# Stores of the w2 and w1 sums moved to ScalarE's queue, w2 loaded in one transfer, and the sums spread anew over the token tiles

## The chip, the cores and the metric

The kernel runs on one core of one Trainium2 chip. That core has five engines, each with an instruction stream of its own that it works through in order: TensorE (PE, with its weight loads shown as PEld), VectorE (DVE), ScalarE (ACT), GpSimd (POOL) and SyncE (SP, which here only issues transfers). Sixteen DMA engines move data between the chip's HBM and the core's SBUF. The metric is the device time of one execution in microseconds.

## The reference, cut to what matters

```python
x = A_x                                   # (1, 2048, 576)
xn = _layernorm(x)
q, k, v = split(xn @ wqkv)                # 32 heads of 18
phi = lambda t: where(t > 0, t + 1, exp(t)) + 1e-6
kv = einsum("bhsd,bhse->bhde", phi(k), v)
z  = einsum("bhsd->bhd", phi(k))
s  = (phi(q) @ kv / (phi(q) . z + 1e-6)) @ wo
g  = silu(gelu(xn @ w1 + b1) @ w2 + b2)   # w1 (576, 4608), w2 (4608, 576)
return x + s * g
```

Everything is float32. The kernel keeps that accuracy by writing each operand as a high part and a low part of a faster 32-bit format and multiplying high by high, high by low and low by high.

## The kernel before: how it is tiled and staged

The work runs in three stages.

**Projection stage** (L547 to L663). A loop over 16 token tiles of 128 tokens. Tile t computes the key columns `pk` (28 products, L315), then adds the outer product of the tile before to the running state (`state`, L381: 10 products into `ps_kva`, `ps_kvb`), then computes the rest of the value columns `pv` (14 products). Tiles 0 to 5 are normalized and transposed on the core. From tile 6 on, transposed x is loaded (`xt`, L260), the tile's mean and scale are stored to HBM by `store_stats` (L264) and read back to all partitions by `load_stats` (`bc`, L269), then POOL subtracts the mean (`center`, L278), DVE multiplies by the scale (`scale`, L281), ACT writes the high part (`set_x_hi`, L289) and DVE the low part (`set_x_lo`, L293, L294). `set_x_hi` of tile t+1 stands in iteration t, and the key products of tile t+1 wait for it. After tile 15 the query weights follow (`split_w` of `wq`, L357, L358, then `query(0)`).

**Attention stage** (L1076 to L1111) and **feed-forward stage** (L1512 to L1609). The feed-forward multiplies with two-level block sums (a Strassen-like scheme), which need sums of blocks of w1 and w2.

Some of those sums are made beside the projection stage, and the change is about these:

- w2 has nine *places* c = 0 to 8, each with four blocks of 128 x 2 x 288 numbers. `w2_load` (L393) brings a place in as two transfers: three blocks in a tile `w2r` (864 KB), the fourth in a tile `w2u` (288 KB), two buffers each.
- Each place has three sums, numbered 5, 6 and 4 and made in that order: `w2_sum` on POOL (L410), the high part by `w2_hi` on ACT (L419), the low part by `w2_lo` on DVE (L423), then `w2_store` (L427) writes both parts, 576 KB, to HBM. The parts stand in a tile `w2o`, of which there are four in turn (`w2slot`), so the high part of a sum waits for the store of the fourth sum before it.
- The last 64 rows of w1 come in five groups q: `we_load` (L439), `we_sums` on POOL (L444), `we_hi` on ACT (L450), `we_lo` on DVE (L454), `we_store` (L458, 896 KB). They use the buffers `w1u` and `w1h`, which later become the x tiles of block 3: `set_x_hi(12)` waits for the last `we_store`.
- Three tables say when. `W2_SUMS[t]` lists the sums that POOL makes at the end of iteration t. Their high and low parts and their stores follow in iteration t+1, the stores at its end. `W2_LOADS[t]` is the place loaded at the end of iteration t. `WE_SUMS` does the same for w1's rows, in iterations 1, 3, 5, 7 and 9.

**What sets the order.** `ordered` (L526) keeps each engine's instructions as written. All transfers are issued from SP, in program order. A transfer of the kernel signals on one of eight completion counters, handed out in turn, and waits before it is issued until the one eight transfers earlier on the same counter has landed. In the built program this is a wait on each transfer's own counter.

## Time and profile before

| | us |
|---|---|
| median of 3 runs | 1112.03 (1110.18 to 1114.05) |
| the profiled execution | 1111.23 |
| its span, from first to last instruction | 1109.4 |
| PE busy | 1092.8 |
| DVE busy | 811.6 |
| ACT busy | 489.1 |
| POOL busy | 453.0 |

The granted TensorE clock was full all through (1.0). The profile's numbers are microseconds from the start of the span. A group row gives engine, line, operation and tiles, then count and durations; "SPq" is SP's queue of issued transfers, whose duration is that of issuing. A waits row reads: engine and line, what it waited for, then total, number of times and the longest. A stretches row gives for each engine the busy time and the number of instructions in it, then the granted clock, the mean busy share of the 16 DMA engines (small overlaps take it over 1) and the rate in GB/s.

### The profile page before, as it was taken

What the parts mean: (1) busy time and instruction counts of PE and PEld (TensorE: products, weight loads), DVE (VectorE), ACT (ScalarE), POOL (GpSimd) and SP (SyncE); (2) the same over time, 40 slices, a digit from 0 to 9 for tenths busy, and PEclk for the clock granted to TensorE, in tenths of its full rate; (3) what the DMA queues carried; (4) which work ended last, traced back from release to release, by engine and by line L of the source; (5) the groups of instructions that cost most, each with busy time, mean ns of one, the idle gap of its engine ahead of it and who ended that gap; (6) DMA issues with size and microseconds to landing.
All of it is one profiled execution on the core that took longest, in us unless ns stands there. A gap on an engine that the chain in (4) does not pass through costs nothing.

```text
span 1109.4 us, 18111 instructions
## 1 busy us (share of the span) xinstructions
PE 1092.8 (98%) x6712; PEld 1008.9 (91%) x6712; DVE 811.6 (73%) x1132; ACT 489.1 (44%) x848; POOL 453.0 (41%) x392
## 2 busy tenths in 40 slices
PE   8998989999999999999999999999999999999998
PEld 8998888999998989989989899898898998989988
DVE  7586667888687888877879788676485674765866
ACT  6654466464554454443544544524233242242342
POOL 3566564232352453534624534325234242341340
PEclk9999999999999999999999999999999999999999
DMA  8799883475879577585585769987766676766452
GB/s 257 254 285 298 279 342 133 142 244 182 293 267 336 195 262 261 188 326 204 210 319 189 284 241 378 403 296 255 232 221 229 207 237 208 248 219 206 140 186 86
DMA packets 90272, 270.17 MB, mean 244 GB/s; under 512 B 11846, under 2 KB 23878, under 8 KB 87496
## 3 DMA queue, kind: packets, MB, share of 16 engines
q1 hardware_dynamic: 90184, 269.02, 70.4%
q8 instruction: 53, 0.87, 0.3%
q14 instruction: 35, 0.29, 0.1%
HBM read 171.28 MB, written 95.76 MB: 241 GB/s over the span
## 4 chain that ended last, share of the span: by engine, by line
PE 87%; DMA 6%; DVE 3%; ACT 1%; issue 1%; POOL 1%; SPq 0%; DVEq 0%; POOLq 0%
PE pm L1287 34%; PE a L1153 10%; PE e L1153 10%; PE zy L1153 10%; PE ps_s L795 5%; PE pq L315 5%; PE b L1153 5%; DMA op<-w2o 2%; PE pd L1403 2%; PE pk L315 1%; DMA bc<-st_dram 1%; DVE w2o L423 1%; PE pv L315 1%; PE ptp L777 1%; DMA w2r<-w 1%
## 5 line engine op out<-in xcount | busy, mean ns | idle before, releaser
L1293 DVE TENSOR_TENSOR macc<-pm,macc 128x576 f32<-128x576 f32 x218 | 163.9, 752 | 54.5 <-PE pm L1287 53.7
L819 ACT CAST h_h<-g 128x512 fp32r<-128x512 f32 x204 | 120.8, 621 | 132.4 <-PE pm L1287 131.3
L822 DVE TENSOR_TENSOR h_l<-g,h_h 128x512 fp32r<-128x512 f32 x204 | 165.0, 816 | 0.0
L1253 POOL TENSOR_TENSOR mid<-g 128x512 f32<-128x512 f32 x34 | 43.9, 1290 | 127.7 <-ACT g L1161 127.7
L1247 POOL TENSOR_TENSOR g<-g 128x512 f32<-128x512 f32 x34 | 55.1, 1622 | 56.6 <-DVE h_l L822 55.3
L1161 ACT ACTIVATE g<-b,b1c 128x512 f32<-128x512 f32 x36 | 24.7, 687 | 116.0 <-DVE b L1179 116.0
L1170 ACT COPY mid<-a 128x512 f32<-128x512 f32 x36 | 21.1, 587 | 117.2 <-PE a L1153 117.2
L865 POOL TENSOR_TENSOR w1raw<-w1raw 128x256 f32<-128x256 f32 x18 | 16.9, 938 | 121.6 <-DVE wa L881 121.6
L1173 DVE TENSOR_TENSOR mid<-b,mid 128x512 f32<-128x512 f32 x36 | 24.7, 687 | 44.6 <-PE b L1153 43.1
L1250 POOL TENSOR_TENSOR g<-g 128x512 f32<-128x512 f32 x34 | 55.2, 1623 | 2.7
L1375 POOL TENSOR_TENSOR fin1l<-fin1h,fin1l 128x288 f32<-128x288 f32 x8 | 6.5, 810 | 118.9 <-DMA fin1l<-s_dram 104.5
L1153 PE MATMUL a<-h0r,wa 128*128 128x512 f32 x144 | 50.4, 390 | 0.0
L1153 PE MATMUL a<-xh,wa 128*128 128x512 f32 x144 | 50.4, 390 | 0.0
L822 DVE TENSOR_TENSOR h_l<-mid,h_h 128x512 fp32r<-128x512 f32 x34 | 48.8, 1437 | 1.2
L1244 POOL TENSOR_TENSOR g<-g 128x512 f32<-128x512 f32 x34 | 46.7, 1372 | 2.7
L1179 DVE TENSOR_TENSOR b<-e,mid 128x512 f32<-128x512 f32 x36 | 25.2, 699 | 30.4 <-PE e L1153 30.4
L760 POOL TENSOR_TENSOR pbuf<-phiq,den 128x576 f32<-128x576 f32 x16 | 19.4, 1211 | 62.2 <-DVE den L759 62.2
L1176 DVE TENSOR_TENSOR mid<-zy,mid 128x512 f32<-128x512 f32 x36 | 24.9, 691 | 24.6 <-PE zy L1153 24.6
L315 PE MATMUL pk<-wkv_h,xh 128*128 128x288 f32 (+1 forms) x160 | 38.4, 322 | 4.4 <-ACT xh L289 3.9
L1161 ACT ACTIVATE g<-e,b1c 128x512 f32<-128x512 f32 x36 | 24.8, 690 | 33.0 <-DVE e L1186 33.0
L1186 DVE TENSOR_TENSOR e<-e,mid 128x512 f32<-128x512 f32 x36 | 24.9, 690 | 19.8 <-PE e L1153 19.8
L315 PE MATMUL pk<-wkv_l,xh 128*128 128x288 f32 (+1 forms) x160 | 38.6, 322 | 0.4 <-POOL wkv_l L358 0.2
(841 smaller groups left out, 3606.1 us busy)
## 6 DMA issues: line engine op xcount, KB each, us to landing
we<-we_dram SPq DMA_DIRECT2D x36, 448.0 KB
op<-w2o SPq DMA_DIRECT2D x27, 576.0 KB
w2raw<-w SPq DMA_DIRECT2D x10, 1152.0 KB
w1raw<-w SPq DMA_DIRECT2D x18, 512.0 KB
op_a<-wa SPq DMA_DIRECT2D x18, 512.0 KB
op_c<-wc SPq DMA_DIRECT2D x18, 512.0 KB
op_d<-wd SPq DMA_DIRECT2D x18, 512.0 KB
wc<-op_c SPq DMA_DIRECT2D x18, 512.0 KB
```

The source lines that it names most:

```text
L315: nc.tensor.matmul(ps[:, h, : ws.stop - ws.start], st, w[:, k, ws], start=(begin and i == 0), stop=(end and i == len(seq) - 1), skip_group ...
L795: nc.tensor.matmul(ps[:, h, :HD], st[:, k, :], w[:, k, h * HD : (h + 1) * HD], start=(i == 0), stop=(i == len(seq) - 1),)
L819: nc.scalar.copy(pair[0], src)
L822: eng.tensor_tensor(pair[1], src, pair[0].bitcast(F32), op=SUB)
L1153: nc.tensor.matmul(ps, st, mv, start=first and n == 0, stop=n == len(seq) - 1, skip_group_check=True,)
L1161: nc.scalar.activation(g, ps, AF.Gelu_apprx_tanh, bias=b1c[:, f : f + 1])
L1244: tt(src[5, pr], A(1, 0), A(1, 1), op=ADD)
L1247: tt(src[6, pr], src[5, pr], A(0, 0), op=SUB)
L1250: tt(src[3, pr], A(0, 1), src[6, pr], op=SUB)
L1253: tt(src[7, pr], A(0, 0), A(1, 0), op=SUB)
L1287: nc.tensor.matmul(ps[:, q, :HD], hs[p][st][:, cs], m[:, p, :], start=(n == 0 and i not in CHAIN), stop=(n == 5), skip_group_check=True,)
L1293: nc.vector.tensor_tensor(dst, src, dst, op=ADD)
```

## The change

Three edits, all in the projection stage. `w2_store` and `we_store` issue from ACT's queue instead of SP's. `w2_load` brings in a place's four blocks with one transfer of 1152 KB into one tile. The tables `W2_LOADS` and `W2_SUMS` are rewritten. Nothing that is computed changes.

```diff
     def w2_load(c):
-        t = w2p.tile([P, 3, 2, HD], F32, tag="w2r", name=f"w2r{c}")
-        nc.sync.dma_start(t.rearrange("p b a d -> p (b a d)"), w2[c][:, D:])
-        u = w2p.tile([P, 2, HD], F32, tag="w2u", name=f"w2u{c}")
-        nc.sync.dma_start(u.rearrange("p a d -> p (a d)"), w2[c][:, :D])
-        w2raw[c] = [t[:, k] for k in range(3)] + [u]
+        t = w2p.tile([P, 4, 2, HD], F32, tag="w2r", name=f"w2r{c}")
+        nc.sync.dma_start(t.rearrange("p b a d -> p (b a d)"), w2[c])
+        w2raw[c] = [t[:, k] for k in range(4)]
 
     def w2_blocks(j):
-        B11, B00, B01, B10 = w2raw[j[0]]
+        B10, B11, B00, B01 = w2raw[j[0]]
...
     def w2_store(j):
         w2_dram[j] = d = dram.tile([P, 2, 2, HD], F32, name=f"op_{j[0]}_{j[1]}")
-        nc.sync.dma_start(d, w2op.pop(j).bitcast(F32))
+        nc.scalar.dma_start(d, w2op.pop(j).bitcast(F32))
...
     def we_store(q):
         src = we["h"][:, : 2 * WB * P].bitcast(F32)
-        nc.sync.dma_start(we_dram[q].rearrange("p v c -> p (v c)"), src)
+        nc.scalar.dma_start(we_dram[q].rearrange("p v c -> p (v c)"), src)
...
-    W2_LOADS = {0: 0, 1: 1, 3: 2, 5: 3, 6: 4, 9: 5, 11: 6, 12: 7, 13: 8}
+    W2_LOADS = {0: 0, 1: 1, 3: 2, 4: 3, 6: 4, 7: 5, 9: 6, 11: 7, 12: 8}
     W2_SUMS = {
-        2: ((0, 5), (0, 6), (0, 4)), 3: ((1, 5),), 4: ((1, 6), (1, 4), (2, 5)),
-        5: ((2, 6), (2, 4)), 6: ((3, 5), (3, 6)), 8: ((3, 4), (4, 5)),
-        10: ((4, 6), (4, 4), (5, 5)), 11: ((5, 6), (5, 4)),
-        12: ((6, 5), (6, 6), (6, 4)), 13: ((7, 5), (7, 6), (7, 4)), 14: ((8, 5), (8, 6), (8, 4)),
+        2: ((0, 5), (0, 6), (0, 4)), 3: ((1, 5), (1, 6), (1, 4)), 4: ((2, 5), (2, 6)),
+        5: ((2, 4), (3, 5)), 6: ((3, 6), (3, 4)), 7: ((4, 5),), 8: ((4, 6), (4, 4)),
+        9: ((5, 5),), 10: ((5, 6), (5, 4), (6, 5)), 11: ((6, 6), (6, 4)), 12: ((7, 5), (7, 6)),
+        13: ((7, 4), (8, 5)), 14: ((8, 6), (8, 4)),
     }
```

## The prediction

> **What bounds the kernel now.** I read the page's head first, then a table of the projection stage by stretches, then the waits of PE, and last the chain of waits inside that stage, since all three edits lie there.

> ```profile
> span 1109.4 us, 18111 instructions
> ...
> core 0: us, PE busy (x) PEld busy (x) DVE busy (x) ACT busy (x) POOL busy (x), PEclk, DMA share, GB/s
> ...
> 58.67:162.37 103.70, 95.50 (x573) 89.26 (x573) 76.34 (x91) 55.00 (x107) 68.85 (x65) 1.00 0.92 301
> ...
> 297.00:1109.40 812.40, 807.57 (x4813) 737.37 (x4811) 593.56 (x802) 326.65 (x552) 312.63 (x251) 1.00 0.69 243
> ```

> From 297 us on PE is busy 807.57 of 812.40 us, and the built programs give PE the same products in the same order, so that part stays. What can move lies between 58.67 and 162.37. One tile's products there, and the query that ends the stretch, cost this much when nothing stalls (pieces of the chain: start, duration):

> ```profile
> 23.35 0.88 PE ps_kva L384 x8
> 24.23 0.18 PE ps_kvb L384 x2
> 24.41 2.92 PE pv L315 x14
> 27.34 4.48 PE pk L315 x28
> ...
> 176.34 3.73 PE pq L315 x28
> ```

> A tile takes 0.88 + 0.18 + 2.92 + 4.48 = 8.46 us; the last stretch, with the query in place of the keys, 7.71. Cut where each state product begins, the stretches are these (the first holds the keys of tile 6, the next of tile 7, and so on; the last the query):

> ```profile
> 58.67:67.39 8.72, 8.61 (x53) 8.08 (x52) 7.84 (x8) 4.99 (x10) 8.56 (x8) 1.00 0.86 281
> 67.39:76.62 9.23, 8.95 (x53) 8.18 (x53) 7.46 (x12) 5.36 (x10) 2.72 (x3) 1.00 1.02 275
> ...
> 93.61:105.37 11.76, 8.98 (x54) 8.08 (x53) 6.98 (x7) 4.49 (x9) 9.45 (x8) 1.00 0.97 275
> 105.37:114.16 8.79, 8.64 (x54) 8.10 (x53) 7.86 (x10) 4.11 (x8) 8.24 (x7) 1.00 0.90 264
> 114.16:124.81 10.65, 9.07 (x52) 8.07 (x52) 6.31 (x8) 4.99 (x10) 7.32 (x5) 1.00 0.63 205
> ...
> 133.39:143.08 9.69, 8.61 (x53) 8.08 (x52) 4.73 (x5) 4.93 (x10) 6.92 (x5) 1.00 1.00 369
> 143.08:151.97 8.89, 8.73 (x52) 8.20 (x53) 7.98 (x7) 5.98 (x13) 6.73 (x5) 1.00 0.97 396
> 151.97:162.37 10.40, 8.34 (x52) 7.63 (x53) 8.73 (x8) 6.29 (x13) 8.87 (x20) 1.00 0.75 295
> ```

> The whole is 103.70 - 10 x 8.46 - 7.71 = 11.4 us over the ideal: tiles 6 and 7 1.03, tile 10 3.30, tile 11 0.33, tile 12 2.19, tiles 14 and 15 1.66, the query 2.69, the rest 0.2. That is the most the change can win. PE's own waits and the chain say why:

> ```profile
> PE pk L315 <- ACT xh L289: 3.9, 2, 2.6
> PE ps_kva L384 <- DVE phik L334: 2.0, 5, 1.1
> PE pq L315 <- ACT wq_h L357: 1.8, 1, 1.8
> ```

> ```profile
> 65.64 8.29 DMA op<-w2o
> ...
> 73.99 8.92 DMA op<-w2o
> 82.93 12.84 DMA bc<-st_dram
> ...
> 99.58 0.73 ACT xh L289
> ...
> 113.46 0.32 SPq L458
> ...
> 138.59 9.49 DMA op<-w2o
> ```

> Tile 10: the load of its mean and scale (`bc`) was issued at 82.93 and landed at 95.77, so its x was ready only at 99.58. It was issued late because SP stood behind stores: each issue waits for the transfer eight before it, and here a store of 65.64 released a store at 73.99, whose landing released `bc`. Tile 12: the last store of w1's rows was issued at 113.46 and x may not enter its buffer before it lands.

> **The change part by part.**

> *Stores on ACT.* 27 + 5 issues leave SP and join ACT.

> ```profile
> L427 SPq DMA_DIRECT2D op<-w2o x27: 319/320/930, 45.6 to 158.6; - x27
> L397 SPq DMA_DIRECT2D w2u<-w x9: 327/518/1238, 12.6 to 142.5; - x9
> ```

> ```profile
> SPq L427 <- DVE w2o L423: 33.8, 18, 6.7
> ...
> ACT xh L289 <- DVE xt L281: 30.9, 9, 8.6
> ...
> 118.91 0.72 ACT L289 CAST xh<-xt 128x640 fp32r<-128x640 f32 x1 [7.57 <-DMA we_dram<-w1h]
> ```

> SP loses 33.8 us of waiting for DVE's low parts. ACT gets 32 x 0.32 = 10.2 us of issuing, two to four at the end of a tile. What is queued behind a store on ACT is the next tile's `set_x_hi`, for which PE waits. The store's wait for the low part costs ACT nothing more, because DVE makes the low part ahead of the `scale` (L281) for which that same `set_x_hi` waits anyway; those 30.9 us also cover the issuing. Without the cover it is 10.2 us on the path. The range per issue is 0.32 to 0.93; no row shows an issue on ACT.

> What the cover does not hold is the eighth-transfer wait. The eight counters are shared by both queues, so an ACT store now waits on ACT for a transfer about one tile older. The worst place is tile 5: its first store waits for tile 4's store of w1's rows, which is behind three sums (3 x 576 + 896 KB = 2.69 MB), while SP loads 256 + 1152 + 288 + 320 + 128 KB = 2.20 MB beside them. Two stretches price 4.89 MB:

> ```profile
> 54.00:57.00 3.00, 3.00 (x20) 2.97 (x19) 3.00 (x3) 0.64 (x3) 1.44 (x1) 1.00 1.07 411
> 57.00:61.00 4.00, 4.00 (x28) 3.91 (x27) 3.14 (x6) 2.23 (x4) 2.96 (x3) 1.00 1.03 106
> ```

> At 411 GB/s 11.9 us, at the stage's mean 301 16.2. Begun at about 60 (the stretch begins at 58.67, and two low parts more than before, 2 x 0.76 by the row further down, stand ahead of the store), it lands at 72 to 76. Two issues (0.64) and `set_x_hi` (0.73) later the keys of tile 7 can start, at 73.4 to 77.6. In the profile tile 6's keys begin at 67.39 - 4.48 = 62.9, so tile 7's are due at 71.4: a stall of 2.0 to 6.2. I take 2.5, near the fast end, since both sides are long rows, and 0.5 for tile 6, whose x comes behind two more low parts (0.76 each below). So tiles 6 and 7 go from 1.0 to 3.0; ends 0 and 6.2.

> Tile 10: in the built order `bc` of tile 10 now has the 1 KB store of a tile's statistics as its eighth predecessor, and no 576 KB store ahead of it in SP. It can leave up to 82.93 - 73.99 = 8.9 us earlier, more than the 3.30 lost. I take 0.3 left; ends 0 and 3.3. SP is not wholly free: its load of w1's next rows and the load of a w2 place still wait for DVE's low parts in the old buffers.

> Tile 12: landing took from 113.46 to the cast at 118.9, 5.4 us. The store was late by what tile 10 had lost, which comes back; but it shares the engines with loads now. Between nothing and 8.92 - 5.4 more than today (5.7), I take 1.2, nearer the low end because DVE's lateness there began with `bc`.

> [...]

> *One transfer for a place.* SP has nine issues less (9 x 0.52 = 4.7 us by L397, off the path, as SP only loads ahead). Sum 5 now waits for 1152 instead of 864 KB: 0.29 MB at 411 GB/s, 0.7 us, on POOL a tile ahead of need; no PE time. If POOL has no slack, 9 x 0.7 = 6.

> *Sums dealt out anew.* The number of sums stays; the durations are

> ```profile
> L410 POOL TENSOR_TENSOR w2r<-w2r x18: 1402/1432/2039, 29.8 to 152.8; 128x576 f32<-128x576 f32 x18
> L423 DVE TENSOR_TENSOR w2o<-w2r,w2o x18: 747/759/2160, 44.8 to 157.0; 128x576 fp32r<-128x576 f32 x18
> ```

> Tile 3 makes three sums instead of one, tile 7 and tile 9 one instead of none, tiles 12, 13 and 14 two instead of three, and the last load moves from tile 13 to 12. In tile 14 three casts in a row needed slots whose stores (138.59, 9.49 us) had just been issued; two per tile leave a tile for the landing: tiles 14 and 15 from 1.66 to 0.4 (0 to 1.7). In the last stretch ACT came late:

> ```profile
> 156.54 0.68 ACT L419 CAST w2o<-w2u 128x576 fp32r<-128x576 f32 x1 [1.23 <-POOL w2u L410]
> ...
> 159.68 1.26 ACT L357 CAST wq_h<-w 128x576 fp32r<-128x576 f32 x2
> ```

> The third cast and the wait before it (0.68 + 1.23 = 1.9) go, and PE waited 1.8 for `wq_h`: the query from 2.69 to 0.3 (0 to 2.7).

> **Sum.** Left over the ideal: 3.0 + 0.3 + 1.2 + 0.4 + 0.3 + 0.5 (tile 11 and the rest) = 5.7, against 11.4. The profiled execution took 1111.23 (1.83 outside the span), so 1111.23 - 5.7 = 1105.5; it stands 0.8 below the median of the runs, so I say 1106.0. All low ends together leave 0.5, or 1100.3; all high ends 3.3 + 5.7 + 1.7 + 2.7 + 6.2 + 0.5 = 20.1, or 1119.9.

> **The rivals.**

> *Transfers are the bound in the middle.* The DMA share is 0.92 over the stage and about 1 in tiles 7 and 10. If a second queue moves nothing faster, tiles 6 to 12 keep their stalls and only the end gains 1.26 + 2.39 = 3.65: 1107.6. Against it: 57 to 61 us shows share 1.03 at 106 GB/s, so a busy share is not full use. [...]

> *The gain at the end is eaten in the middle.* Tiles 6 and 7 at 6.2 and tile 12 at 3.5 with the rest as above: 11.2 left, 1111.0. For it: store landings of 8 to 9 us are as long as a tile.

> *ACT is paced by its own stores: slower.* In most tiles from 5 to 13 the built order makes a tile's first store wait for a store of the tile before. A tile then cannot be shorter than a landing plus two issues. With 9.49 + 0.64 = 10.13 that is 1.67 over the ideal in nine tiles, 15.0, plus 0.7 for the end: 15.7 left, 4.3 more than now, 1115.5. It decides once landings pass 8.46 - 0.64 = 7.8 us, and costs time against now when they average over about 9. For it: the three landings above. Against it: those were behind SP's loads in one queue, and after a stall the transfers catch up.

> **How the numbers follow.** Forecast 0.44, transfers bound 0.13, eaten 0.20, paced by stores 0.23. The forecast's own range is 1101 to 1109. A measurement tells about 0.3% (3.3 us) from no change. The forecast is nearly all faster; transfers bound lies at the edge: faster 0.53, same 0.24, slower 0.23. Range 1101 to 1115, which reaches to the low half of the slower case.

> **What would show it.** Right: the tile 10 stretch near 8.5, `bc` issued before 78, the last stretch under 8.2, ACT waits on transfers of 2 to 3 us ahead of stores in tile 5. Wrong: ACT waiting before stores in every tile, or stretches of 9 to 10 us throughout; or SP still issuing `bc` of tile 10 after 82.

## The result and the profile after

| | before | after |
|---|---|---|
| median of the runs, us | 1111.78 (1109.25 to 1114.05, 6 runs) | 1117.98 (1114.64 to 1120.92, 6 runs) |
| the profiled execution, us | 1111.23 | 1120.05 |
| its span, us | 1109.4 | 1118.3 |

The changed kernel is slower by 0.56%: the ratio of its time to the time before is 1.0056, with a 95% interval of 1.0031 to 1.0081. By the medians that is 6.2 us; the two profiled executions, read below, lie 8.8 us apart, so they show the loss somewhat larger than it commonly is. Line numbers after `w2_load` are lower by two (`set_x_hi` keeps L289; `w2_hi` is L417, `w2_store` L425, `we_store` L456).

I read the stretches first. The columns are those of the table of stretches in the prediction; the view is that of the changed kernel, cut where the projection stage's part and the attention stage end:

```profile
core 0 of [0], span 1118.3 us
...
58.10:171.19 113.09, 99.99 (x573) 93.36 (x572) 75.02 (x95) 55.20 (x109) 67.86 (x65) 0.95 0.89 295
171.19:305.82 134.63, 134.08 (x989) 129.73 (x988) 104.01 (x154) 73.27 (x125) 45.21 (x36) 1.00 0.56 185
305.82:1118.30 812.48, 807.58 (x4813) 737.41 (x4811) 591.56 (x802) 326.72 (x552) 312.70 (x251) 1.00 0.69 243
```

The last row was 812.40 us before and the middle one 134.63 as now, so all of the loss lies in the first. That stretch was 103.70 us and is 113.09: 9.4 more. PE is busy 4.5 us longer there (99.99 against 95.50) with the same 573 products, at a granted clock of 0.95; the other 4.9 is waiting. Cut at each state product, as in the prediction (keys of tile 6 first, the query last), the changed kernel shows:

```profile
58.10:71.89 13.79, 10.79 (x53) 9.66 (x52) 10.37 (x17) 6.08 (x13) 4.62 (x4) 0.88 1.02 325
71.89:83.23 11.34, 8.96 (x53) 7.98 (x52) 6.99 (x8) 5.29 (x10) 9.45 (x9) 1.00 1.01 303
83.23:93.38 10.15, 10.15 (x53) 9.71 (x53) 8.36 (x16) 5.23 (x10) 4.30 (x4) 0.83 1.02 392
93.38:101.85 8.47, 8.47 (x53) 8.22 (x52) 5.21 (x10) 4.16 (x8) 5.25 (x8) 1.00 1.03 259
101.85:113.15 11.30, 9.03 (x54) 7.98 (x53) 7.90 (x7) 4.42 (x9) 9.76 (x9) 1.00 0.80 252
113.15:123.93 10.78, 8.73 (x54) 8.19 (x53) 9.85 (x11) 4.69 (x9) 9.67 (x7) 1.00 0.97 286
123.93:135.41 11.48, 10.45 (x52) 9.47 (x53) 5.31 (x8) 4.99 (x10) 5.59 (x4) 0.85 0.46 165
135.41:146.44 11.03, 8.67 (x53) 8.14 (x52) 3.94 (x7) 4.51 (x9) 4.37 (x3) 1.00 1.02 359
146.44:155.01 8.57, 8.57 (x52) 8.32 (x53) 6.47 (x9) 6.30 (x12) 4.98 (x4) 1.00 1.01 363
155.01:163.49 8.48, 8.48 (x54) 8.22 (x53) 8.43 (x8) 5.63 (x11) 8.12 (x11) 1.00 0.88 316
163.49:171.19 7.70, 7.70 (x53) 7.46 (x52) 2.18 (x3) 3.92 (x8) 1.74 (x10) 1.00 0.56 214
```

The end of the stage now runs at the ideal (8.46 a tile, 7.71 for the query), so of the 4.35 us lost in tiles 14, 15 and the query only 0.1 are left. Tiles 6 to 13 lose 20.7 us, against 7.0 before. The waits between 58 and 172 us (engine and line, what it waited for, then total, times, longest) say where to look:

```profile
ACT xh L289 <- DVE xt L281: 13.6, 6, 4.3
ACT xh L289 <- DMA we_dram<-w1h: 10.2, 1, 10.2
...
PE ps_kva L384 <- DVE phik L334: 6.5, 3, 2.4
...
ACT xh L289 <- DMA xt<-xT: 6.4, 1, 6.4
...
ACT xh L289 <- DMA bc<-st_dram: 6.3, 1, 6.3
...
ACT xh L289 <- DMA op<-w2o: 4.7, 1, 4.7
...
PE pk L315 <- ACT xh L289: 4.0, 4, 1.5
```

Before, `set_x_hi` (xh L289) waited for its own data, DVE's scaled x, and once for a buffer. Now it also waits for loads and stores that it doesn't read: it stands behind an issue on ACT's queue, and that issue waits for the transfer eight before it. ACT's timeline around tile 7 (start, duration, then in brackets the idle time before), and DVE's row for the same x:

```profile
73.22 2.24 ACTq L425 DMA_DIRECT2D op<-w2o  x2
75.50 0.73 ACT L289 CAST xh<-xt 128x640 fp32r<-128x640 f32 x1 [6.42 <-DMA xt<-xT]
```

```profile
71.14 0.82 DVE L281 TENSOR_TENSOR xt<-xt,bc 128x640 f32<-128x640 f32 x1
```

Tile 7's x was scaled at 71.96 and cast at 75.50: 3.5 us late. Tile 6's was scaled at 62.23 and cast at 64.33.

A waits row gives the transfer that the profile takes to have ended an idle time; the chain of waits and the completion counter that the trace keeps with each issue say more exactly what an issue on ACT waited for. The last store ahead of tile 6's cast waited for an older store (issued 48.20, landed 63.88). The last store ahead of tile 7's cast waited for SP's load of a transposed x, and the one ahead of tile 10's for SP's load of a tile of x, as the chain shows (start, duration):

```profile
64.51 10.55 DMA xt<-xT
...
92.99 12.90 DMA x<-x
```

So the row with `bc` above, 6.3 us, is the hold by that second load. The counters are shared by both queues: here stores on ACT waited for SP's loads (the two above, of 10.55 and 12.90 us) as well as for other stores.

The hold reaches PE by two paths. One is x: PE waits 4.0 us in all for `set_x_hi`. The other is phi of the keys, which stands on ACT and DVE behind that cast and behind the sums' high and low parts: PE waits 6.5 us for it, in tiles 7, 11 and 13. In tile 7 it waited only 0.25 us for x, but then 2.12 us for phi, up to 83.23. In tile 13 phi stood behind a high part that waited 5.5 us for its slot.

### The profile page after: what moved, and what is told of

Its sections match the earlier page's. It is cut to its first block, busy times and chain, and to the rows that moved or that the text cites. A ratio compares the mean times of both kernels' runs of the same rounds, so it can differ in the third digit from the quotient of the medians.

```text
span 1118.3 us, 18097 instructions
## 1 busy us (share of the span) xinstructions
PE 1097.2 (98%) x6712; PEld 1013.0 (91%) x6712; DVE 805.3 (72%) x1132; ACT 489.3 (44%) x848; POOL 454.4 (41%) x392
## 4 chain that ended last, share of the span: by engine, by line
PE 88%; DMA 6%; DVE 3%; issue 1%; ACT 1%; SPq 0%; POOL 0%; ACTq 0%; DVEq 0%
PE pm L1285 34%; PE a L1151 10%; PE e L1151 10%; PE zy L1151 10%; PE pq L315 5%; PE ps_s L793 5%; PE b L1151 5%; PE pd L1401 2%; PE pk L315 2%; DMA bc<-st_dram 1%; PE pv L315 1%; DMA x<-x 1%; DMA xt<-xT 1%; DMA w2r<-w 1%; DMA op<-w2o 1%
## 5 line engine op out<-in xcount | busy, mean ns | idle before, releaser
L408 POOL TENSOR_TENSOR w2r<-w2r 128x576 f32<-128x576 f32 x27 | 44.7, 1656 | 30.1 <-DMA w2r<-w 25.6
L1373 POOL TENSOR_TENSOR fin1l<-fin1h,fin1l 128x288 f32<-128x288 f32 x8 | 6.5, 808 | 118.9 <-DMA fin1l<-s_dram 76.0
L315 PE MATMUL pk<-wkv_h,xh 128*128 128x288 f32 (+1 forms) x160 | 39.4, 329 | 4.5 <-ACT xh L289 4.0
L315 PE MATMUL pk<-wkv_l,xh 128*128 128x288 f32 (+1 forms) x160 | 39.2, 327 | 0.4 <-POOL wkv_l L358 0.3
```

Source lines behind the costliest of these rows:

```text
L315: nc.tensor.matmul(ps[:, h, : ws.stop - ws.start], st, w[:, k, ws], start=(begin and i == 0), stop=(end and i == len(seq) - 1), skip_group ...
L408: nc.gpsimd.tensor_tensor(dst, a, b, op=SUB)
```

## Experiments

The table gives for the main runs what each tile's stretch lost over the ideal (its length minus 8.46, for the query minus 7.71, cut at the state products of that run's profiled execution), in us. It is one execution of each. Each run was timed beside the kernel before, whose median lay between 1110.69 and 1114.47 us from one occasion to the next, so runs are compared by their ratios to it and not by their medians. "New tables" are those of the changed kernel.

| run | 6 | 7 | 8 | 9 | 10 | 11 | 12 | 13 | 14 | 15 | query | sum |
|---|---|---|---|---|---|---|---|---|---|---|---|---|
| before | .3 | .8 | .1 | 0 | 3.3 | .3 | 2.2 | .1 | 1.2 | .4 | 2.7 | 11.4 |
| after | 5.3 | 2.9 | 1.7 | 0 | 2.8 | 2.3 | 3.0 | 2.6 | .1 | 0 | 0 | 20.8 |
| e1: new tables, one load | 0 | 3.2 | 1.7 | 2.1 | 1.7 | 0 | 9.8 | 0 | 0 | 0 | 0 | 18.3 |
| e2: stores on ACT alone | 0 | 8.9 | 0 | 4.0 | 0 | 0 | 2.3 | 1.7 | 1.8 | 1.9 | 1.4 | 22.1 |
| e3: one load alone | 0 | 0 | .4 | 0 | 0 | 0 | 7.3 | 0 | 0 | .6 | 4.9 | 13.1 |
| e4: new tables alone | 0 | 3.2 | 1.7 | 3.0 | 3.0 | 0 | 8.2 | 0 | 0 | 0 | 0 | 19.1 |
| e8: e4 with fewer bytes | .4 | 1.1 | .1 | 1.0 | .8 | 2.6 | 1.7 | 0 | 0 | 0 | 0 | 7.6 |
| e12: tables late, one load | 0 | 0 | .1 | 0 | 5.9 | 2.3 | 0 | 0 | 0 | 0 | 0 | 8.3 |
| e13: e12, stores on ACT | 0 | 5.1 | 0 | 6.2 | 0 | .7 | .2 | 4.3 | 1.7 | 0 | 0 | 18.1 |
| e16: e12, phi first | 0 | 0 | 0 | 0 | 0 | 1.5 | 0 | 0 | 0 | 0 | .3 | 1.6 |

**Each edit by itself.** Four kernels: the changed one with `w2_store` and `we_store` back on SP (e1), and the one before with one edit each.

```diff
-        nc.scalar.dma_start(d, w2op.pop(j).bitcast(F32))
+        nc.sync.dma_start(d, w2op.pop(j).bitcast(F32))
```

> The changed kernel with the stores back on SP's queue: one transfer for a place and the new tables stay. Theory A (on ACT the stores' waits for the transfer eight before them stand ahead of set_x_hi, x comes late, PE stalls, and three stalls are followed by 3.4 us of half clock): the end keeps its gain (the last three stretches near 8.5, 8.5 and 7.7 us), the middle goes back to about 7 us over the ideal, no half clock: about 1107.5 us. Theory B (the new tables put too many transfers into tiles 3 to 7, whichever queue issues the stores): tiles 6 to 8 stay several us over the ideal, 1115 to 1118 us.

> The kernel before with only the stores moved to ACT's queue; two transfers for a place and the old tables stay. Theory A: the middle stalls as in the changed kernel and the end is not helped: 1116 to 1122 us, half clock in places, ACT's set_x_hi waiting on transfers for over 20 us in all. Theory B: within 3 us of the kernel before.

> The kernel before with only the one transfer of 1152 KB for a place. Theory A and theory B: within 2 us of the kernel before. Theory C (the larger transfer delays the sums, and what stands behind it in SP's queue): 1115 us or more.

> The kernel before with only the new tables of loads and sums; stores on SP and two transfers for a place stay. Theory A: like the run with the stores back on SP, about 1107.5 us, the gain all in the last three stretches. Theory B: 1115 to 1118 us, with tiles 6 to 8 several us over the ideal.

| run | median, us | ratio to before | 95% interval |
|---|---|---|---|
| e1 | 1117.08 | 1.0026 | 1.0012 to 1.0041 |
| e2 | 1120.65 | 1.0056 | 1.0036 to 1.0075 |
| e3 | 1113.49 | 0.9999 | 0.9986 to 1.0012 |
| e4 | 1117.86 | 1.0033 | 1.0018 to 1.0048 |

Neither theory A (the tables cost nothing) nor B (the stores cost nothing) holds alone: each of the two edits costs by itself, and together they cost no more than the worse one. C falls: one load for a place is worth nothing on its own.

In e2, ACT's timeline and DVE's (same columns as above) show the hold with nothing else changed:

```profile
67.23 8.57 ACTq L427 DMA_DIRECT2D op<-w2o  x2
75.90 0.72 ACT L289 CAST xh<-xt 128x640 fp32r<-128x640 f32 x1 [10.52 <-DMA op<-w2o]
```

```profile
66.80 1.30 DVE L281 TENSOR_TENSOR xt<-xt,bc 128x640 f32<-128x640 f32 x1
76.65 0.82 DVE L293 TENSOR_TENSOR xl<-xt,xh 128x512 fp32r<-128x512 f32 x1 [8.55 <-ACT xh L289]
```

Tile 7's scaled x was there at 68.1. ACT spent 67.23 to 75.80 issuing two stores and cast x 7.8 us late. The row puts the wait down to a store, but the second store carries the counter of SP's load of a w2 place, issued at 64.57. POOL, whose next sum reads that load, starts when it has landed, together with ACT's second issue at 75.47:

```profile
75.53 3.23 POOL L410 TENSOR_TENSOR w2r<-w2r 128x576 f32<-128x576 f32 x2 [3.02 <-DMA w2r<-w]
```

A second profiled execution of the same kernel gave 1118.18 us and the same picture: 7.2 us lost in tile 7, 3.4 in tile 9, `set_x_hi` waiting 10.6 us behind the same two stores. (Its label names an edit which that run does not have.)

> The kernel before with the stores alone on ACT, once more, for the stretches of a second profiled execution. If ACT is held by its stores, set_x_hi again waits 5 us or more for transfers in tiles 7 and 9, and the stage loses 8 to 12 us against the kernel before; if the first execution was a chance, the stage loses under 4.

**Why the new tables cost.** In e4 the stores are on SP, and no store stands ahead of `set_x_hi`. Its chain of waits (start, duration of each piece) goes through transfers, each released by the one before:

```profile
61.39 13.79 DMA xt<-xT
75.25 7.84 DMA st_dram<-mv
83.11 10.33 DMA xt<-xT
93.45 10.83 DMA xt<-xT
104.35 13.50 DMA op<-w2o
117.91 10.83 DMA we_dram<-w1h
```

The last is the store of w1's last rows, which empties the buffer that tile 12's x needs. It took 10.8 us where before it took 5.4, and PE waited 6.6 us for that x. Another 6.0 us PE waited for phi, in tiles 7 and 9: in tile 7 phi stands behind the high part of a sum for whose place POOL had waited 7.2 us. To separate bytes from work, e8 kept e4's tables and all work of POOL, DVE and ACT, and halved the bytes of 15 stores.

```diff
+        n = 1 if j[0] < 5 else 2
-        nc.sync.dma_start(d, w2op.pop(j).bitcast(F32))
+        nc.sync.dma_start(d[:, :n], t[:, :n])
```

> The kernel before with the new tables alone, in which the stores of the 15 sums of places 0 to 4 write only the high part (288 KB instead of 576 KB); their low parts are stored at the end of tile 15, from other data, so the time of the whole is not to be compared and the output is not the reference's. POOL's, DVE's and ACT's work is the same. Theory 'backlog': the bytes are what is late; the excess of tiles 6 to 13 falls from 19 us to under 8. Rival 'work': the low parts and sums dealt anew stand ahead of x on DVE, ACT and POOL; it stays above 14.

The stage's row of the table of stretches in e4, and then in e8:

```profile
57.22:168.61 111.39, 98.82 (x574) 94.75 (x573) 66.91 (x92) 54.31 (x105) 64.67 (x65) 0.92 0.95 290
```

```profile
57.67:157.56 99.89, 95.39 (x573) 90.94 (x572) 75.55 (x94) 53.45 (x105) 67.38 (x64) 0.98 0.91 286
```

11.5 us of the 19.1 go with 4.3 MB (15 x 288 KB). So the tables cost by transfers that are late, and not by the engines' work. The new tables move bytes ahead and add none, while e8 takes away bytes that the kernel before moves too; how much of the 11.5 us is due to the moving alone it doesn't show.

**Moving the stores behind x on ACT.** e5 is the changed kernel with ACT's stores issued behind the next tile's `set_x_hi`.

```diff
                 set_x_hi(t + 1), set_x_lo(t + 1)
+            if t != 10 + 1:
+                late_stores(t)
...
-        for j in W2_SUMS.get(t - 1, ()):
-            w2_store(j)
+        if t + 1 < NTR or last:
+            for j in W2_SUMS.get(t - 1, ()):
+                w2_store(j)
```

> The changed kernel, with ACT's stores put behind the next tile's set_x_hi in ACT's order (in iteration 11 they stay ahead of it, since tile 12's x uses the buffer that the last store of w1's rows empties). Same transfers, same tables. Theory 'ACT is held': the store's wait for the transfer eight before it no longer stands ahead of set_x_hi, so the stalls of tiles 6, 7 and 10 (5.33, 2.88 and 2.84 us) fall below 1 each unless the tables alone cause them, and the time is that of the kernels with the new tables and SP's stores or less, 1112 to 1117. Theory 'the transfers only': x comes late because the transfers are late, whoever waits; the time stays 1117 to 1120.

1126.37 us, ratio 1.0135 (1.0112 to 1.0157), 27.4 us lost in the stage: a miss. The edit has a seam. The stores at the end of iteration 4 stayed where they were, ahead of tile 6's `set_x_hi`, now with the store of w1's rows first among them, and that cast waited 8.26 us. From then on each store is issued later, and so should land later for whatever waits eight transfers behind. The run doesn't separate the two theories.

**Taking x off ACT.** e15 is e2 with the high part of x made on DVE.

```diff
-        nc.scalar.copy(h[:, :, cs], xt)
+        nc.vector.tensor_copy(h[:, :, cs], xt)
```

> The kernel before with the stores alone on ACT, and the high part of x (set_x_hi) made on DVE instead of ACT, so that it stands behind no store; DVE gets 0.7 us more in a tile. Theory 'ACT is held, and x with it': most of the 6 to 9 us that the stores on ACT cost come back, 1111 to 1115. Rival 'the hold costs through all of ACT's work': the exponentials of the keys stand behind the same stores, and the time stays 1116 to 1121.

1114.42 us, ratio 1.0028 (1.0016 to 1.0039): half of e2's 0.56%, though the two intervals just overlap. ACT is held by the same stores, and phi behind them is late. ACT's and PE's timelines around tile 7:

```profile
65.93 6.66 ACTq L427 DMA_DIRECT2D op<-w2o  x3
```

```profile
78.64 2.07 PE L384 MATMUL ps_kva<-phik,vb 128*127 128x126 f32 x8 [3.79 <-DVE phik L334]
```

Tile 7's x was cast on DVE at 66.62, ahead of need, and PE still lost 3.95 us in the tile, 3.79 of it waiting for phi. So both readings hold in part. The cast's extra 0.8 us a tile on DVE is in what is left too, and no run separates it.

**The half clock.** e7 fills four stalls of the changed kernel with products that nobody reads (`FILL_S` stands ahead of the state product in the same way).

```diff
+    FILL_K, FILL_S = {6: 6, 10: 5}, {7: 8, 11: 8}
+            for _ in range(FILL_K.get(t, 0)):
+                nc.tensor.transpose(pk[:, 0, HD : HD + P], ident, ident)
```

> The changed kernel, with 27 transposes of the identity on PE whose result nobody reads: 6 ahead of tile 6's key products, 8 ahead of the state product of iteration 7, 5 ahead of tile 10's keys, 8 ahead of the state product of iteration 11, each group shorter than the stall that it lies in. Theory 'half clock': PE idle for about 2 us of a 3.41 us window brings one window at half clock, 1.7 us lost each time; with the stalls filled, the granted clock of the stage is 1.00 and the time 3 to 5 us lower, 1113 to 1115. Rival 'the clock is no loss of its own': the next x is late anyway and the time lost at half clock would be waited; 1117 to 1119, with clock 1.00 and longer stalls.

1115.80 us, ratio 1.0047 (1.0029 to 1.0065), 17.4 us lost in the stage instead of 20.8. The clock is 1.00 in tiles 6 to 11; tile 12, whose stall is longer in this execution and unfilled, is at 0.89. The median is 2.2 us lower than the changed kernel's, but against the kernel before the ratio fell only from 1.0056 to 1.0047, which is 1.0 us, and the two intervals overlap: a net cost of the half clock is not shown.

**Other tables.** The gain at the end needs two sums a tile from tile 12 on; the new tables pay for it with sums and loads moved ahead all through tiles 3 to 9. e6 keeps the old table through tile 6 and spreads the rest evenly. e9 and e10 also sum w1's last group a tile earlier; e10 adds nothing in tile 7. e12 is e10 with one load for a place. Stores are on SP in all four. The edit of e10 (and e12), lines that are new:

```diff
+    WE_SUMS = {1: 0, 3: 1, 5: 2, 7: 3, 8: 4}
+    W2_LOADS = {0: 0, 1: 1, 3: 2, 5: 3, 6: 4, 9: 5, 10: 6, 11: 7, 12: 8}
...
+        9: ((4, 6), (4, 4)), 10: ((5, 5), (5, 6), (5, 4)), 11: ((6, 5), (6, 6), (6, 4)),
+        12: ((7, 5), (7, 6)), 13: ((7, 4), (8, 5)), 14: ((8, 6), (8, 4)),
```

> The kernel before, with its own tables through tile 6, two sums in tiles 7 and 8, and the new tables from tile 9 on (loads of places 5, 6, 7, 8 after tiles 8, 9, 11, 12). Stores on SP, two loads for a place. Theory 'backlog': what costs in the new tables is that tiles 3 to 5 store three, two and two sums and load a place each, which leaves transfers over for tiles 7 to 12; here that is gone and the gain of tiles 14, 15 and the query (4.3 us) stays, so 1105 to 1110. Rival 'any even spread costs': two sums in every tile from 7 on delay tile 12's buffer in the same way; 1113 to 1118.

> The kernel before with its own tables through tile 6, then two sums in most tiles and never three after tile 11, and w1's last group summed in tile 8 instead of 9, so that its store leaves a tile earlier. Stores on SP, two loads for a place. Theory 'tile 12's buffer': in the runs with the sums spread, tile 12 loses 7 to 10 us because its x uses the buffer of the last store of w1's rows; with the store one tile (8.5 us) earlier that falls below 2 and the gain of the end (4.3 us) shows in the time: 1104 to 1109. Rival 'the transfers are full': the share of the DMA engines is 1.0 in tiles 7 to 11, so whatever is moved ahead comes back as a stall elsewhere: 1111 to 1116.

> As the run before, but with nothing added in tile 7: two sums in tile 9, three each in 10 and 11, two each from 12 on. Theory 'tile 12's buffer': 1104 to 1109, since tiles 7 and 8 keep what they have before. Rival 'the transfers are full': three stores and a load of a place in each of iterations 11 and 12 bring stalls of 3 us or more there; 1111 to 1116.

> The kernel before with three edits: the sums spread late as in the run before last, w1's last group a tile earlier, and a place of w2 in one transfer. One transfer less for each place moves the eighth-transfer wait to an older transfer. If that helps SP where tile 10's mean and scale leave late (4.16 us lost there with two loads), 1105 to 1109; if one load for a place is worth nothing, as it was alone, 1108 to 1111, the time of the two-load form.

| run | median, us | ratio to before | 95% interval | tile 12 lost, us |
|---|---|---|---|---|
| e6 | 1113.41 | 1.0022 | 1.0009 to 1.0035 | 8.0 |
| e9 | 1110.03 | 0.9990 | 0.9977 to 1.0003 | 0.1 |
| e10 | 1109.30 | 0.9985 | 0.9973 to 0.9997 | 1.1 |
| e12 | 1106.01 | 0.9947 | 0.9933 to 0.9960 | 0.0 |

Tile 12's loss goes with the earlier store, as theory said, but e9 and e10 hardly gain: e9 loses 3.8 us in tile 9 and 3.8 in tile 10, e10 4.2 in tile 10. With one load for a place the version beats both kernels. One transfer less for each place moves the eighth-transfer wait to an older transfer; that this is the reason was not tested. What it still lost, tile 10, its ACT timeline shows: the high part of w1's last group waits for the store of the group before it, one tile back, out of the same buffer, and phi stands behind.

```profile
102.49 0.94 ACT L448 CAST w1h<-w1u 128x896 fp32r<-128x896 f32 x1 [6.74 <-DMA we_dram<-w1h]
103.33 0.65 ACT L328 ACTIVATE ek<-pk 128x576 f32<-128x576 f32 x1
```

e14 puts two tiles between the last groups, e16 puts phi ahead of all sums, e17 ahead of w1's sums alone.

```diff
+            k_t, _ = phi(t1, pk, f"k{t}", values)
             for j in sums2:
                 w2_hi(j)
...
-            k_t, _ = phi(t1, pk, f"k{t}", values)
```

> The faster kernel of the run before last in this series (sums spread late, one load for a place, stores on SP), with w1's groups summed in tiles 1, 2, 4, 6, 8 instead of 1, 3, 5, 7, 8. There tile 10 lost 5.92 us and tile 11 2.27, as ACT's high part of the last group waited 6.7 us for the store of the group before it, one tile earlier, out of the same buffer. With two tiles between the last groups that wait should be under 2 and the time 1100 to 1104; if the wait was not what held tile 10, or if it comes back at tile 3, where groups 0 and 1 follow each other, 1105 to 1109.

> The fastest kernel so far (sums spread late, w1's last group in tile 8, one load for a place, stores on SP), with phi of the tile's keys moved ahead of the high and low parts of all sums from tile 5 on, on ACT and DVE. In that kernel tile 10 lost 5.92 and tile 11 2.27 us, as phi of tile 9 stood behind a high part of w1's sums that waited 6.7 us for a store. If that is the cause, both go and the time is 1097 to 1101. If the sums, now behind phi's wait for PE, come later and their stores with them, other stalls take the place: 1104 to 1110.

> As the run before, but phi is ahead of w1's sums only and stays behind the sums of w2. Theory as there: tiles 10 and 11 lose under 1 us together, 1097 to 1101. Rival: DVE's low part of w1's sums, now later, makes the next store of them and with it tile 12's x late; 1103 to 1108.

e14: 1107.94 us (ratio 0.9975, 0.9965 to 0.9985): phi of tile 7 now stands behind sums whose load came late, 5.7 us in tile 8. e17: 1106.07 us (0.9952, 0.9935 to 0.9968): tiles 6 to 10 are clean, 4.2 us are lost in tile 11. e16: 1103.87 us (0.9932, 0.9917 to 0.9947), the lowest, though its interval overlaps those of e12 and e17; its profiled execution, 1100.62 us, lies below the other five, which took 1103.48 to 1104.55. In that execution only 1.6 us of the stage's 11.4 are left:

```profile
57.44:151.39 93.95, 93.05 (x573) 89.52 (x572) 78.28 (x90) 54.76 (x107) 66.76 (x58) 1.00 0.96 328
```

**The stores on ACT again, without the backlog.** e13 is e12 with its stores on ACT: the changed kernel with other tables.

> The faster kernel of the run before (sums spread late, w1's last group early, one load for a place), with the stores of the sums moved to ACT's queue again: the changed kernel with other tables. Theory 'ACT is held': with the backlog of the tables gone, the stores on ACT still cost by themselves what they cost beside the old tables (about 6 to 9 us), 1111 to 1116. Rival 'only the tables were at fault': the stores land sooner here, ACT waits little, and the time stays 1105 to 1108.

1117.24 us, ratio 1.0056 (1.0044 to 1.0068), where e12 has 0.9947: 1.1% more, about 12 us. ACT's timeline shows e2's picture once more (tile 7's x was scaled at 67.2):

```profile
63.81 8.65 ACTq L425 DMA_DIRECT2D op<-w2o  x3
72.56 0.73 ACT L289 CAST xh<-xt 128x640 fp32r<-128x640 f32 x1 [10.28 <-DMA op<-w2o]
```

By its counter the third store waited for SP's `bc` load, issued at 57.99 and landed at 72.06. With these tables it is the stores on ACT that keep the change from gaining. Whether stores on ACT with counters of their own would be harmless was not tried.

## Why the prediction was wrong

**What bounds the kernel** was read rightly. All of the difference lies in the stage named. Of the 11.4 us that it was said could be won at most, e16's profiled execution wins 9.8; by the medians e16 wins 7.2.

The sum forecast 5.7 us left over the ideal and 20.8 were measured. Of the 15.1 us between them, tiles 6 and 7 account for 5.2, tile 10 for 2.5, tile 12 for 1.8, and tiles 8, 9, 11 and 13, for which 0.5 was put down, for 6.1; the end was 0.6 better than forecast. The sum of all high ends, 1119.9, would have held the result; the range was ended at 1115.

**Stores on ACT** is the first step that failed, by its size and by its path. The mechanism was named, ACT held by the eighth-transfer wait ahead of `set_x_hi`, but the prediction looked for it in tile 5 alone. There it was nearly right: the store of w1's rows landed at 73.14, inside the 72 to 76 forecast, and tile 7 lost 2.9 us against 2.5. Part of that is luck: PE lost it waiting for phi and not for x, and with the stores on SP the new tables lose 3.2 in the same tile (e4). The same wait held the last store at the end of tile 4 until 63.96, and tile 6, forecast at 0.5, lost 5.3, of which 3.0 are PE's waits; the half clock followed. Neither edit alone loses anything there (e2, e4). Tiles 6 and 7 together lose 8.2 against 3.0 forecast and 6.2 at most. The wait came back with both other tables, where the transfer eight before was still under way: two stores took ACT 8.57 us in e2 (the old tables) and three 8.65 us in e13 (the late ones), each time behind one of SP's loads. And the path had only x in it: phi stands behind the same issues, and PE waited 6.5 us for phi against 4.0 for x, though not all of the 6.5 lay behind an issue. On the kernel before the stores on ACT alone cost 0.56% (e2), on e12 1.1% (e13). The 10.2 us of issuing cost little, as forecast: an issue on ACT takes 0.33 us when it does not wait.

**Tile 10** was forecast at 0.3 and lost 2.8. Its `bc` did leave earlier for its tile: SP's timeline of the changed kernel has

```profile
85.77 0.84 SPq L269 DMA_DIRECT2D bc<-st_dram  x1
```

16.1 us ahead of the state product at 101.85, where before it was 10.7 (82.93 to 93.61). So the sign set in advance, `bc` issued after 82, was met but meant nothing: the whole schedule had shifted. The load itself was no quicker here with stores on the other queue; POOL's timeline has the first use of it,

```profile
100.16 1.59 POOL L278 TENSOR_TENSOR xt<-xt,bc 128x640 f32<-128x640 f32 x1 [3.14 <-DMA bc<-st_dram]
```

14.4 us after the issue, where before 12.84 us passed to its landing. DVE and ACT of the changed kernel show what took the gain:

```profile
101.79 2.01 DVE L281 TENSOR_TENSOR xt<-xt,bc 128x640 f32<-128x640 f32 x1 [0.25 <-POOL xt L278]
```

```profile
105.96 0.33 ACTq L456 DMA_DIRECT2D we_dram<-w1h  x1
106.39 0.72 ACT L289 CAST xh<-xt 128x640 fp32r<-128x640 f32 x1 [6.31 <-DMA bc<-st_dram]
```

x was scaled at 103.8, before PE was due at its keys (101.85 + 3.98 = 105.83), and ACT was held until 106.3 by the issue of a store of w1's rows, which waited for SP's load of x (92.99, 12.90, shown above). What SP no longer waits for, ACT waits for.

**Tile 12** (1.2 forecast, 0 to 5.7) lost 3.0, inside its bounds.

**Sums dealt out anew** is the second step that failed, by a term that was not there. It priced only the end: 0.4 for tiles 14 and 15 and 0.3 for the query, measured 0.1 and 0.0. The sums and loads moved ahead into tiles 3 to 9 were given no price at all; e4 shows ratio 1.0033 with the gain of the end already in it, and e8 that it goes with the bytes. Tiles 11 and 13, in no term but the 0.5 for the rest, lose 4.9, nearly all of it in PE's waits for phi (2.05 and 2.36 us).

**One transfer for a place** at nothing was right here (e3). With e10's tables it was worth about 0.4% (0.9985 to 0.9947), which the forecast had no reason to see.

**The clock** had no term. PE is busy 4.5 us more for the same products; tile 8's 1.7 us are half clock and nothing else. What the clock costs net is open (e7).

**The rivals.** "Paced by its own stores" had the right sign at 1115.5 and, with ACT held by the eighth-transfer wait, half of the mechanism: SP's loads hold ACT too. It had the shape wrong: tiles 9, 14 and 15 are at the ideal, and the loss comes in a few long holds and not as 1.67 us in each of nine tiles. As to bandwidth, two queues were no faster here than one: the stage's mean was 295 GB/s, and 301 before. What decided here was another thing: the wait before the issue moved to the engine that issues (2.24 us for the two stores ahead of tile 7's cast).

## What to carry to other kernels

The stores issued from ACT brought their waits with them, and not only 0.33 us of issuing each (two took 8.57 us in e2): look at which older transfer such an issue must wait for, and at what stands behind it on that engine. When work is dealt out anew, add up the bytes of each stretch and not only the instructions: with 4.3 MB less to store and the same work, 11.5 of the 19.1 us lost with the new tables were gone (e8). And what stands behind a wait matters as much as the wait: putting phi ahead of the sums' casts (e16, 0.9932) left almost no stalls in its profiled execution, while setting w1's groups further apart to shorten the wait (e14, 0.9975) lost against e12 (0.9947).

## What the hardware showed that I had not expected

```profile
142.13:145.54 3.41, 1.95 (x13) 1.66 (x11) 0.76 (x1) 2.67 (x6) 1.21 (x2) 1.00 1.02 410
145.54:148.95 3.41, 2.51 (x17) 2.41 (x18) 2.53 (x3) 2.28 (x6) 2.93 (x2) 1.00 1.08 314
63.64:67.05 3.41, 1.56 (x8) 1.27 (x9) 1.94 (x2) 2.52 (x5) 2.83 (x2) 1.00 1.02 379
67.05:70.46 3.41, 3.41 (x14) 3.33 (x13) 3.35 (x6) 2.00 (x6) 0.58 (x1) 0.50 1.01 427
80.71:84.12 3.41, 1.28 (x11) 1.00 (x10) 3.38 (x5) 0.11 (x1) 2.98 (x2) 1.00 1.05 257
84.12:87.53 3.41, 3.41 (x13) 3.10 (x12) 2.58 (x4) 2.38 (x5) 2.66 (x2) 0.50 1.02 409
121.67:125.08 3.41, 1.36 (x13) 1.16 (x11) 3.41 (x3) 0.00 (x0) 3.41 (x3) 1.00 0.73 115
125.08:128.49 3.41, 3.41 (x11) 3.06 (x11) 0.22 (x1) 0.00 (x0) 3.33 (x3) 0.50 0.94 389
```

The stretch ahead of each slow one has PE idle for 1.85 to 2.13 of its 3.41 us, and the starts of the slow ones lie 5 and 12 times 3.41 us apart. PE's stall of 2.36 us ahead of 146.44 falls across two stretches of that grid (1.46 and 0.90 us idle), and no slow one follows. So, as an estimate from a clock of 0.50 over 3.41 us, a stall of about 2 us costs up to 1.7 us more if it falls into one such stretch. The other runs agree. In the 16 runs with half clock in this stage, the one above among them, I laid a grid of 3.41 us through each run's own slow stretches. Between 55 and 165 us PE was idle for 1.85 us or more in 31 stretches at full clock, and a stretch at half clock followed every time; it was idle for 1.67 us or less in 418, and none followed. At 1.68 one followed and at 1.72 it did not, so in these runs the line lay at about half of the stretch.
